# The first two x tiles of a gated two-branch attention kernel: loaded through the DMA crossbar instead of transposed on TensorE, with fewer weight loads and a longer warm-up

## The chip, the cores and the metric

The kernel runs on one core of one Trainium2 chip. The metric is the device time of one execution in microseconds (us). Every execution lists its time, its span and its mean granted TensorE clock, which is given to three digits. On one core no execution here is marked slow; all of those compared are listed as fast.

Each call of experiments ran on one chip together with the kernel before, and kernels are compared within a call.

## The reference, cut to what matters

```python
x = A_x                                    # 1 x 2048 x 1024, bf16
g = sigmoid((x * gate_w).sum(-1, keepdims=True))
a = A_ref(x, A_wqkv, A_wo)                 # linear attention, 32 heads of 32
b = B_ref(x, B_wqkv, B_wo)                 # dilated local attention
return g * a + (1 - g) * b

# in A_ref:
qkv = x @ wqkv
pq, pk = phi(q), phi(k)                    # phi(t) = where(t > 0, t + 1, exp(t)) + 1e-6
```

Only the start matters here: the first work is `pk = phi(x @ wk)` of branch A. The contraction is over the 1024 columns of x, so TensorE needs x transposed: `xT`, with these columns on the partitions.

## The kernel before

x is cut into 16 tiles of 128 rows. Tiles 2 to 15 are transposed by the DMA crossbar on their way in. Tiles 0 and 1 are loaded as rows and transposed on TensorE. The first half of the key weights (`WkA[0]`, 1 MB) comes in eight loads of 128 KB that alternate between two issuing queues, those of SyncE and ScalarE.

```python
load_rows(nc.sync, 0, 1)                   # x tile 0, as rows, 256 KB
load_rows(nc.scalar, 1, 2)                 # x tile 1
WkA = [wpool.tile([P, KT, 512], BF16, name="WkA0", tag="wa")]
for kt in range(KT):                       # KT = 8
    (nc.scalar if kt % 2 else nc.sync).dma_start(out=WkA[0][:, kt, :], in_=A_wqkv[kt * P:(kt + 1) * P, D:D + 512])
for t in range(2, NB):                     # NB = 16
    nc.sync.dma_start_transpose(out=xT[:, :, t * P:(t + 1) * P], in_=rows(x, t * P, (t + 1) * P))
WkA += load_w("WkA", A_wqkv, D, "wa", only=(1,))     # second weight half, 1 MB
load_rows(nc.sync, 2, 4)
...                                        # more rows of x, more weights
warm_up(28)                                # 128x128 matmuls on constants
for t in range(2):
    tp = ps_1.tile([P, KT, P], BF16, name="xt_ps", tag="p1")
    for kt in range(KT):
        nc.tensor.transpose(out=tp[:, kt, :], in_=xrow[:, t, kt * P:(kt + 1) * P], identity=ident[:])
    nc.vector.tensor_copy(out=xT[:, 0:4, t * P:(t + 1) * P], in_=tp[:, 0:4, :])
    nc.scalar.copy(out=xT[:, 4:8, t * P:(t + 1) * P], in_=tp[:, 4:8, :])
warm_up(6)
...
for half in range(2):                      # the projection, L178
    for t0, n in [(0, 2)] + [(t, 1) for t in range(2, NB)]:
        pj = [ps_1.tile([P, 512], F32, name="pk_ps", tag="p1") for _ in range(n)]
        for kt in range(KT):
            for i in range(n):
                t = t0 + i
                nc.tensor.matmul(pj[i][:], lhsT=xT[:, kt, t * P:(t + 1) * P], rhs=WkA[half][:, kt, :],
                                 start=(kt == 0), stop=(kt == KT - 1))
        ...                                # phi of each tile
```

The *next stage* below is `g_ps` (L203): x rows times pk, 256 matmuls. (The expectations call it the third stage.)

Of the kernel before, what the change touches and what calls it, by code (L numbers as in the profile page):

```python
# [7 lines left out]

ACT = mybir.ActivationFunctionType
ALU = mybir.AluOpType  # L10
BF16 = mybir.dt.bfloat16
F32 = mybir.dt.float32
PE = mybir.EngineType.PE
DVE = mybir.EngineType.DVE
P = 128
# [26 lines left out]
def kernel(  # L42
# [11 lines left out]
    nc = tc.nc  # L54
    S, D = A_x.shape[1:]
    assert D == 1024 and S == 2048

    x = A_x[0].rearrange("(m two) d -> two m d", two=2)
    out2 = out[0].rearrange("(m two) d -> two m d", two=2)

    def rows(ap, s0, s1):
        return ap[s0 // 1024, s0 % 1024:(s1 - 1) % 1024 + 1, :]
# [3 lines left out]
    KT = D // P  # L66
    NB = S // P
# [7 lines left out]
    consts = ctx.enter_context(tc.tile_pool(name="consts", bufs=1))  # L75
    wpool = ctx.enter_context(tc.tile_pool(name="wpool", bufs=2))
    dram = ctx.enter_context(tc.tile_pool(name="dram", bufs=1, space=bass.MemoryType.DRAM))
    big = ctx.enter_context(tc.tile_pool(name="big", bufs=1))
# [3 lines left out]
    def load_w(name, src, col0, tag, only=(0, 1)):  # L82
        halves = []
        for h in only:
            w = wpool.tile([P, KT, 512], BF16, name=f"{name}{h}", tag=tag)
            c0 = col0 + h * 512
            nc.sync.dma_start(out=w[:], in_=src[:, c0:c0 + 512].rearrange("(kt p) n -> p kt n", p=P))
            halves.append(w)
        return halves

    xT = big.tile([P, KT, S], BF16, name="xT", tag="xT")
    xrow = big.tile([P, NB, D], BF16, name="xrow", tag="vV")

    def load_rows(eng, t0, t1):
        eng.dma_start(out=xrow[:, t0:t1, :], in_=rows(x, t0 * P, t1 * P).rearrange("(t p) d -> p t d", p=P))

    load_rows(nc.sync, 0, 1)
    load_rows(nc.scalar, 1, 2)
    WkA = [wpool.tile([P, KT, 512], BF16, name="WkA0", tag="wa")]
    for kt in range(KT):  # L100
        (nc.scalar if kt % 2 else nc.sync).dma_start(out=WkA[0][:, kt, :], in_=A_wqkv[kt * P:(kt + 1) * P, D:D + 512])
    for t in range(2, NB):
        nc.sync.dma_start_transpose(out=xT[:, :, t * P:(t + 1) * P], in_=rows(x, t * P, (t + 1) * P))
    WkA += load_w("WkA", A_wqkv, D, "wa", only=(1,))
    load_rows(nc.sync, 2, 4)
    for t in range(4, NB, 4):
        load_rows(nc.sync, t, t + 4)
    WvA = load_w("WvA", A_wqkv, 2 * D, "wb")
# [2 lines left out]
    WqA = load_w("WqA", A_wqkv, 0, "wa")  # L111


    ident = consts.tile([P, P], BF16, name="ident")
    make_identity(nc, ident[:])
    onesb = consts.tile([P, P], BF16, name="onesb")
    nc.vector.memset(onesb[:], 1.0)
    bdmask = consts.tile([P, P], F32, name="bdmask")
# [24 lines left out]
    def phi(dst, pj):  # L143
        e = work.tile([P, 512], F32, name="e", tag="e")
        nc.scalar.activation(out=e[:], in_=pj[:], func=ACT.Exp)  # L145
        nc.vector.tensor_scalar(out=e[:], in0=e[:], scalar1=1.0, scalar2=1e-6, op0=ALU.min, op1=ALU.add)  # L146
        nc.vector.scalar_tensor_tensor(out=dst, in0=pj[:], scalar=0.0, in1=e[:], op0=ALU.max, op1=ALU.add)

    with tc.manual_schedule(engines={PE}):

        with ExitStack() as s1:
            ps_1 = s1.enter_context(tc.tile_pool(name="ps_1", bufs=6, space=bass.MemoryType.PSUM))
            junk = s1.enter_context(tc.tile_pool(name="junk", bufs=1))


            def warm_up(n):
                warm = ps_1.tile([P, P], F32, name="warm", tag="p1")
                for i in range(n):
                    nc.tensor.matmul(warm[:], lhsT=onesb[:], rhs=onesb[:], start=True, stop=True)

            warm_up(28)
            for t in range(2):
                tp = ps_1.tile([P, KT, P], BF16, name="xt_ps", tag="p1")
                for kt in range(KT):
                    nc.tensor.transpose(out=tp[:, kt, :], in_=xrow[:, t, kt * P:(kt + 1) * P], identity=ident[:])  # L165
                nc.vector.tensor_copy(out=xT[:, 0:4, t * P:(t + 1) * P], in_=tp[:, 0:4, :])
                nc.scalar.copy(out=xT[:, 4:8, t * P:(t + 1) * P], in_=tp[:, 4:8, :])
            warm_up(6)

            s1.enter_context(tc.manual_schedule(engines={DVE}))  # L170
            pk = big.tile([P, NB, D], BF16, name="pk", tag="pkO")
            for half in range(2):
                for t0, n in [(0, 2)] + [(t, 1) for t in range(2, NB)]:
                    pj = [ps_1.tile([P, 512], F32, name="pk_ps", tag="p1") for _ in range(n)]
                    for kt in range(KT):
                        for i in range(n):
                            t = t0 + i
                            nc.tensor.matmul(pj[i][:], lhsT=xT[:, kt, t * P:(t + 1) * P], rhs=WkA[half][:, kt, :],  # L178
                                             start=(kt == 0), stop=(kt == KT - 1))
                    for i in range(n):  # L180
                        phi(pk[:, t0 + i, half * 512:(half + 1) * 512], pj[i])

            zacc = junk.tile([P, D], F32, name="zacc", tag="zacc")
            gw_row = junk.tile([P, D], BF16, name="gw_row", tag="gw")
# [12 lines left out]
            for half in range(2):  # L197
                g_ = kq.tile([P, KT, 512], BF16, name=f"G{half}", tag="kq")
                G.append(g_)
                for kt in range(KT):  # L200
                    pj = ps_1.tile([P, 512], F32, name="g_ps", tag="p1")
                    for t in range(NB):
                        nc.tensor.matmul(pj[:], lhsT=xrow[:, t, kt * P:(kt + 1) * P],  # L203
                                         rhs=pk[:, t, half * 512:(half + 1) * 512],
                                         start=(t == 0), stop=(t == NB - 1))
# [12 lines left out]
            for c in range(KT):  # L218
                kvp = ps_1.tile([P, P], F32, name="kv_ps", tag="p1")
                for kt in range(KT):  # L220
                    nc.tensor.matmul(kvp[:], lhsT=WvA[c // 4][:, kt, (c % 4) * P:(c % 4 + 1) * P],  # L221
                                     rhs=G[c // 4][:, kt, (c % 4) * P:(c % 4 + 1) * P],
                                     start=(kt == 0), stop=(kt == KT - 1))
                nc.vector.tensor_tensor(out=KVT[:, c, :], in0=kvp[:], in1=bdmask[:], op=ALU.mult)
            for half in range(2):
                zp = ps_1.tile([P, 512], F32, name="z_ps", tag="p1")
                for i in range(2):
                    nc.tensor.matmul(zp[:], lhsT=onesb[:], rhs=zhl[:, i, half * 512:(half + 1) * 512],  # L228
                                     start=(i == 0), stop=(i == 1))
# [300 lines left out]
```

## Time and profile before

| | before |
|---|---|
| median of three executions | 494.51 us (494.06 to 494.51) |
| span of the profiled execution | 493.0 us |
| first projection matmul starts | 7.51 us |
| granted clock rises to full | 10.38 us |
| first projection of the second weight half starts | 36.56 us |
| first weights of the next stage loaded into PE | 63.97 us |

In the views PE is TensorE, PEld its weight loads, DVE VectorE, ACT ScalarE, POOL GpSimd and SP SyncE; a q behind a name means the engine's instruction queue, for instance while it issues a transfer. L178 is line 178 of the kernel, and x16 counts instructions. Engines wait on semaphores, counters that a finished instruction or transfer raises.

The page of the kernel before: busy time of each engine with its share of the span and its instructions, and the engines of the chain of work that ended last.

```profile
PE 487.6 (99%) x3350; PEld 232.0 (47%) x3350; DVE 283.3 (57%) x550; ACT 181.9 (37%) x281; POOL 7.9 (2%) x28
...
PE 98%; DMA 1%; ACT 0%; issue 0%; ACTq 0%
```

TensorE is the limit from one end to the other. Only the start, where it still waits for data, can give something. The chain of the kernel before in its first 66 us: first the shares by line, then the pieces as start, length and what.

```profile
by line: PE pk_ps L178 85.8%; DMA xrow<-in_A_x_dram 6.6%; PE xt_ps L165 2.9%; PE g_ps L203 2.6%; PE warm L159 1.0%; issue 0.2%
...
0.80 4.34 DMA xrow<-in_A_x_dram
5.14 0.05 issue
5.19 1.89 PE xt_ps L165 x16
7.08 0.64 PE warm L159 x6
7.72 56.63 PE pk_ps L178 x256
```

A load, 16 transposes, six warm-up matmuls, then projections without a gap. The timeline of PE in the kernel before (start, length, what, and in brackets the idle time before it and what ended it):

```profile
1.12 3.17 PE L159 MATMUL warm<-onesb 128*128 128x128 bf16 x28 [1.12 <-DVE onesb L117]
5.19 1.89 PE L165 MATMUL xt_ps<-ident,xrow 128*128 128x128 bf16 x16 [0.91 <-DMA xrow<-in_A_x_dram]
6.87 0.85 PE L159 MATMUL warm<-onesb 128*128 128x128 bf16 x6
7.51 29.21 PE L178 MATMUL pk_ps<-WkA_77,xT 128*128 128x512 bf16 x128
36.56 27.79 PE L178 MATMUL pk_ps<-WkA_100,xT 128*128 128x512 bf16 x128
```

The two halves have the same 128 matmuls, yet the first takes 29.21 us and the second 27.79. The weight loads into PE (PEld) in the kernel before show where the 1.4 us are:

```profile
8.37 0.15 PEld L178 LDWEIGHTS <-xT 128*128 128x128 bf16 x1 [0.27 <-issue]
8.79 0.15 PEld L178 LDWEIGHTS <-xT 128*128 128x128 bf16 x1 [0.27 <-issue]
...
10.45 1.61 PEld L178 LDWEIGHTS <-xT 128*128 128x128 bf16 x8 [0.22 <-issue]
```

Up to 10.45 us a projection starts every 0.43 us, afterwards every 0.216 us: the clock is at half until its rise at 10.38 us. The trace holds that rise. The clock changes on a grid of windows of 3.41 us. Busy time of each engine in stretches of one window, counted back from the rise, in the kernel before (columns: PE, PEld, DVE, ACT and POOL busy us with instructions, PEclk, DMA share, GB/s; the PEclk column gives 1.00 ahead of the first recorded change too, so it is of no use here):

```profile
0.14:3.55 3.41, 2.43 (x24) 2.44 (x25) 0.65 (x6) 1.28 (x1) 2.93 (x18) 1.00 0.41 96
3.55:6.97 3.42, 2.51 (x24) 2.25 (x23) 0.42 (x1) 0.25 (x1) 1.37 (x7) 1.00 0.90 298
6.97:10.38 3.41, 3.41 (x15) 1.61 (x13) 0.42 (x1) 0.92 (x2) 0.00 (x0) 1.00 1.14 165
```

PE was busy for 71%, 73% and 100% of the three windows.

### The profile page before, as it was taken

The page shows a single profiled execution, that of the slowest core. Times are in us where ns is not written, and L with a number is a line of the kernel's source. Part 1 is how long each engine was busy: PE and PEld are TensorE (multiplying, and loading weights), DVE is VectorE, ACT ScalarE, POOL GpSimd, SP SyncE. Part 2 cuts the span into 40 slices and gives each one's busy share as a digit, 9 for nine tenths or more (in the row PEclk, how much of TensorE's full clock was granted, in tenths as well). Part 3 has the DMA queues.
Part 4 walks back from the last instruction along what each step waited for, and adds up shares of the span by engine and source line. Part 5 has one row for each costly group of instructions (what it writes and reads, how often), then busy time and mean ns, then how long its engine had stood idle before and what let it go on. Part 6 is the DMA issues. An engine that isn't in the chain of part 4 may idle for free.

```text
span 493.0 us, 8254 instructions
## 1 busy us (share of the span) xinstructions
PE 487.6 (99%) x3350; PEld 232.0 (47%) x3350; DVE 283.3 (57%) x550; ACT 181.9 (37%) x281; POOL 7.9 (2%) x28
## 2 busy tenths in 40 slices
PE   8999999999999999999999999999999999999997
PEld 5444444446444444444444545454544444444444
DVE  1766689941328999997476767676765397000000
ACT  1333311121543333332455655655655333112121
POOL 3000000000200000000000000000000000000000
PEclk9999999999999999999999999999999999999999
DMA  8999950000621222236011133111164832110101
GB/s 192 163 277 368 348 167 0 1 0 13 206 76 47 93 93 83 66 122 199 3 36 30 32 88 57 30 36 30 36 134 92 208 85 68 60 43 33 43 33 43
DMA packets 78293, 46.03 MB, mean 93 GB/s; under 512 B 51632, under 2 KB 72240, under 8 KB 78256
## 3 DMA queue, kind: packets, MB, share of 16 engines
q1 hardware_dynamic: 77536, 44.73, 33.6%
q10 hardware_dynamic: 720, 0.79, 0.6%
q8 instruction: 26, 0.43, 0.4%
q14 instruction: 11, 0.09, 0.1%
HBM read 21.23 MB, written 7.34 MB: 58 GB/s over the span
## 4 chain that ended last, share of the span: by engine, by line
PE 98%; DMA 1%; ACT 0%; issue 0%; ACTq 0%
PE kq_ps L339 23%; PE d_ps L458 21%; PE pk_ps L178 11%; PE p_ps L262 11%; PE g_ps L203 11%; PE p_ps L296 8%; PE q_ps L296 2%; DMA xrow<-in_A_x_dram 1%; PE kv_ps L221 1%; PE q_ps_4385 L458 1%; PE q_ps L458 1%; PE p_ps L251 1%; PE xt_ps L165 0%; PE q_ps_4266 L296 0%; PE q_ps_4165 L296 0%; PE z_ps L228 0%
## 5 line engine op out<-in xcount | busy, mean ns | idle before, releaser
L203 PE MATMUL g_ps<-pk,xrow 128*128 128x512 bf16 x256 | 55.4, 379 | 0.0
L146 DVE TENSOR_SCALAR e<-e 128x512 f32<-128x512 f32 x64 | 27.2, 424 | 39.9 <-ACT e L145 39.9
L463 ACT ACTIVATE osb<-d_ps,omg 128x512 bf16<-128x512 f32 (+1 forms) x31 | 20.9, 673 | 72.5 <-PE d_ps L458 64.2
L178 PEld LDWEIGHTS <-xT 128*128 128x128 bf16 x256 | 25.4, 99 | 31.0 <-issue 1.8
L458 PEld LDWEIGHTS <-OBT 128*128 128x128 bf16 x264 | 25.7, 98 | 29.2
L203 PEld LDWEIGHTS <-xrow 128*128 128x128 bf16 x256 | 25.0, 98 | 30.2
L262 PEld LDWEIGHTS <-xT 128*128 128x128 bf16 x256 | 25.0, 98 | 30.2
L296 PEld LDWEIGHTS <-xT 128*128 128x128 bf16 x256 | 24.2, 98 | 28.0
L378 DVE TENSOR_TENSOR PT_1893<-PT_1893,mask 128x672 bf16<-128x672 bf16 (+3 forms) x42 | 23.7, 571 | 18.1 <-ACT PT_1893 L376 17.7
L339 PE MATMUL kq_ps<-xT,WkB_1071 128*128 128x512 bf16 x128 | 32.9, 380 | 0.0
L339 PE MATMUL kq_ps<-xT,WqB_1876 128*128 128x512 bf16 x128 | 32.9, 379 | 0.0
L145 ACT ACTIVATE e<-pk_ps 128x512 f32<-128x512 f32 x32 | 18.9, 597 | 37.9 <-PE pk_ps L178 37.9
L339 PE MATMUL kq_ps<-xT,WkB_1069 128*128 128x512 bf16 x128 | 32.3, 379 | 0.0
L339 PE MATMUL kq_ps<-xT,WqB_1874 128*128 128x512 bf16 x128 | 32.2, 379 | 0.0
L378 DVE TENSOR_TENSOR PT_1894<-PT_1894,mask 128x672 bf16<-128x672 bf16 (+3 forms) x40 | 22.3, 565 | 16.8 <-ACT PT_1894 L376 16.5
L345 DVE CAST kqt<-kq_ps 128x512 bf16<-128x512 f32 x32 | 22.0, 687 | 16.5 <-PE kq_ps L339 16.5
L262 PE MATMUL p_ps<-WvB_114,xT 128*128 128x512 bf16 x128 | 30.9, 379 | 0.0
L262 PE MATMUL p_ps<-WvB_116,xT 128*128 128x512 bf16 x128 | 30.9, 379 | 0.0
L458 PEld LDWEIGHTS <-pqT_4443 128*128 128x128 bf16 x200 | 19.6, 98 | 22.1
L267 ACT CAST tmp<-p_ps 128x512 bf16<-128x512 f32 x32 | 18.8, 587 | 30.3 <-PE p_ps L262 30.3
L178 PE MATMUL pk_ps<-WkA_77,xT 128*128 128x512 bf16 x128 | 29.2, 392 | 0.0
L458 PE MATMUL d_ps<-WoB_4080,OBT 128*128 128x512 bf16 (+1 forms) x128 | 28.5, 366 | 0.0
(399 smaller groups left out, 673.6 us busy)
## 6 DMA issues: line engine op xcount, KB each, us to landing
out_dram<-osb SPq DMA_DIRECT2D x31, 128.0 KB, 1.9
xrow<-in_A_x_dram SPq DMA_DIRECT2D x3, 1024.0 KB, 12.0
pqd<-tmp SPq DMA_DIRECT2D x12, 256.0 KB, 2.0
V<-tmp SPq DMA_DIRECT2D x4, 264.0 KB, 2.5
WkA_100<-in_A_wqkv_dram SPq DMA_DIRECT2D x1, 1024.0 KB, 7.2
WvA_106<-in_A_wqkv_dram SPq DMA_DIRECT2D x1, 1024.0 KB, 14.6
WvA_108<-in_A_wqkv_dram SPq DMA_DIRECT2D x1, 1024.0 KB, 15.3
WoA_110<-in_A_wo_dram SPq DMA_DIRECT2D x1, 1024.0 KB, 13.1
```

Source lines behind the costliest of these rows:

```text
L145: nc.scalar.activation(out=e[:], in_=pj[:], func=ACT.Exp)
L146: nc.vector.tensor_scalar(out=e[:], in0=e[:], scalar1=1.0, scalar2=1e-6, op0=ALU.min, op1=ALU.add)
L178: nc.tensor.matmul(pj[i][:], lhsT=xT[:, kt, t * P:(t + 1) * P], rhs=WkA[half][:, kt, :], start=(kt == 0), stop=(kt == KT - 1))
L203: nc.tensor.matmul(pj[:], lhsT=xrow[:, t, kt * P:(kt + 1) * P], rhs=pk[:, t, half * 512:(half + 1) * 512], start=(t == 0), stop=(t == NB - 1))
L262: nc.tensor.matmul(st["pj"][:], lhsT=xT[:, kt, t * P:(t + 1) * P], rhs=WvB[half][:, kt, :], start=(kt == 0), stop=(kt == KT - 1))
L267: nc.scalar.copy(out=v[:, half * 16:(half + 1) * 16, 0:Dh], in_=st["pj"][:].rearrange("p (h e) -> p h e", h=16))
L296: nc.tensor.matmul(st["pj"][:], lhsT=xT[:, kt, t * P:(t + 1) * P], rhs=WqA[half][:, kt, :], start=(kt == 0), stop=(kt == KT - 1))
L339: nc.tensor.matmul(st["pj"][:], lhsT=W[c // 4][:, kt, (c % 4) * P:(c % 4 + 1) * P], rhs=xT[:, kt, cols], start=(kt == 0), stop=(kt == KT - 1))
L345: nc.vector.tensor_copy(out=kqt[:, 1, cols], in_=st["pj"][:])
L378: nc.vector.tensor_tensor(out=ptv[:, hs], in0=ptv[:, hs], in1=m[:, None, :].broadcast_to([P, 2, W_]), op=ALU.mult)
L458: nc.tensor.matmul(st["ps"][:, 0:n], lhsT=lhsT, rhs=W[c0 // 512][:, c, c0 % 512:c0 % 512 + n], start=(side == 0 and c == 0), stop=(side == ...
L463: nc.scalar.activation(out=osb[:, 0:n], in_=st["ps"][:, 0:n], func=ACT.Copy, scale=omg[:, tb:tb + 1])
```

## The change

The intent: take the 16 TensorE transposes and their four copies off the start. Tile 0 comes through the crossbar as the very first transfer, tile 1 between the second and the third quarter of the weights, all on one queue. The weights come in four loads of 256 KB. The projections are ordered as the data should arrive: four of tile 0, four of tile 1, then two each. The warm-up grows from 28 to 36 matmuls. The rows of x for tiles 0 and 1, which the next stage needs, move behind the second weight half.

```diff
-    load_rows(nc.sync, 0, 1)
-    load_rows(nc.scalar, 1, 2)
     WkA = [wpool.tile([P, KT, 512], BF16, name="WkA0", tag="wa")]
-    for kt in range(KT):
-        (nc.scalar if kt % 2 else nc.sync).dma_start(out=WkA[0][:, kt, :], in_=A_wqkv[kt * P:(kt + 1) * P, D:D + 512])
+    nc.sync.dma_start_transpose(out=xT[:, :, 0:P], in_=rows(x, 0, P))
+    for i in range(4):
+        if i == 2:
+            nc.sync.dma_start_transpose(out=xT[:, :, P:2 * P], in_=rows(x, P, 2 * P))
+        nc.sync.dma_start(out=WkA[0][:, 2 * i:2 * i + 2, :],
+                          in_=A_wqkv[2 * i * P:(2 * i + 2) * P, D:D + 512].rearrange("(kt p) n -> p kt n", p=P))
     for t in range(2, NB):
         nc.sync.dma_start_transpose(out=xT[:, :, t * P:(t + 1) * P], in_=rows(x, t * P, (t + 1) * P))
     WkA += load_w("WkA", A_wqkv, D, "wa", only=(1,))
-    load_rows(nc.sync, 2, 4)
+    load_rows(nc.sync, 0, 4)
 ...
-            warm_up(28)
-            for t in range(2):
-                ...  # 8 transposes and 2 copies
-            warm_up(6)
 ...
+            warm_up(36)
+            first = [ps_1.tile([P, 512], F32, name="pk_ps", tag="p1") for _ in range(2)]
+            for t, kts in ((0, (0, 1, 2, 3)), (1, (0, 1, 2, 3)), (0, (4, 5)), (1, (4, 5)), (0, (6, 7)), (1, (6, 7))):
+                for kt in kts:
+                    project(first[t], t, kt, 0)
+                if kts[-1] == KT - 1:
+                    phi(pk[:, t, 0:512], first[t])
```

The rest of the diff drops the identity matrix and rewrites the loop of the other tiles. After the first 16 projections PE executes the same instructions in both kernels, and in the same order but for the first 16 projections of the second weight half: there the kernel before alternates between tiles 0 and 1, and the changed one takes them one after the other. It costs nothing that can be seen (27.79 and 27.80 us for the second half).

## The prediction

> **What bounds the kernel now.** TensorE. The page gives PE 487.6 us busy of a span of 493.0 (99%), and the chain of work that ended last is 98% PE. Only the head can move. There the chain of waits reads: 0.80 to 5.14 us the DMA of the first x rows, 5.19 to 7.08 the 16 transposes on PE, 0.64 us of warm-up matmuls, then from 7.51 us projection matmuls without a gap. After the first two x tiles PE's instruction order is the same in both kernels.
>
> A second limit in the head is the clock. The timeline shows the first projections 0.427 us apart until 10.45 us, then about 0.214. The recorded clock rises to full at 10.38 us, one window of 3.41 us after 6.97. PE's busy time was 2.43 us in 0.14 to 3.55, 2.51 in 3.55 to 6.97, and all of 3.41 in 6.97 to 10.38: only the full window released it. The Trainium skill ("TensorE: Matmul & The Clock Gate", Part 1) describes this: half clock until a busy window of about 3.4 us, free-running. This trace agrees.
>
> **What goes, comes, moves.** Gone: 16 PE transposes (1.89 us), two DVE and two ACT copies (0.42 and 0.58 us each), eight 128 KB weight loads on two queues. Added: two crossbar loads and 8 warm-up matmuls. A crossbar load costs 1.31 us of issue; from issue to landing took 3.9 us at best, 4.5 in the median. The weights become four 256 KB loads, in line behind the first crossbar load. The x rows (0.5 MB) move behind the second weight half.
>
> Estimates from these durations. First crossbar load issued 0.8, landed about 4.9. Quarters 1 and 2 issued from 2.1, landed about 5.6 and 6.4. The second crossbar load is issued at about 3.1, queues behind them, and lands about 8.0 (7.3 to 8.6). Quarters 3 and 4 land about 9.0 and 9.8.
>
> So projections start at about 5.6 instead of 7.51 us, four of them for tile 0, still at half clock; they end about 7.3. Then PE waits about 0.7 us for the second tile. That gap falls into the window 6.97 to 10.38.
> - If the window counts as busy anyway: about 9.6 projections are done at 10.38 instead of 6.7, a gain of 2.9 x 0.214 = 0.6 us. About 45%.
> - If it doesn't: the clock rises at 13.8 us, with about 17.6 projections done instead of 22.7, a loss of 1.1 us. About 55%.
>
> **Critical path.** All 1.9 us of transposes lay on it, yet most of what they free is given back to the wait for the second tile and to the half clock. Later x tiles come every 1.5 us and are used every 1.71; tile 2 should land about 11 us and be needed about 11.8. The second weight half landed at 34.6 and was needed at 36.6; I expect about 34 to 36, so at most some tenths of waiting.
>
> **Prediction: 494.6 us, range 493.0 to 496.0.** Faster by over 2%: 0.5%. Within 2%: 99%. Slower by over 2%: 0.5%.
>
> **What would show each step.** First projection at 5.3 to 6.2 us, released by a DMA. A PE gap of 0.3 to 1.2 us after the fourth projection, ended by the second crossbar load. Time of the clock's rise: 10.4 (gain) or about 13.8 (loss). No other PE gap before 36 us.
>
> **What would make it wrong.** Crossbar and plain loads in one queue slowing each other, so that tile 1 or tile 2 lands over 1 us late; the second weight half late; or a crossbar load of a cold queue landing much before 4.9 us with the clock released early, a gain of 1.5 us or more.

## The result, and the profile after

| | before | after |
|---|---|---|
| median of six executions | 494.51 us (494.06 to 495.10) | 493.09 us (492.66 to 494.60) |
| ratio | | 0.9975 (95% interval 0.996 to 0.999) |
| span of the profiled execution | 493.0 us | 491.1 us |
| first projection | 7.51 us | 5.81 us |
| clock rises | 10.38 us | 6.05 us |
| second weight half, first projection | 36.56 us | 34.92 us |
| next stage, first weights into PE | 63.97 us | 62.34 us |
| last matmul ends | 489.66 us | 488.03 us |

A ratio is the mean time of one kernel's fast runs over that of the other's of the same rounds, so it is not quite the ratio of the medians. The change is within 2%, and faster by 1.4 us. Two further calls gave 0.998 each. The changed kernel has a median of 493.20 us in 18 executions. The two profiled executions took 494.82 and 492.92 us, one above its kernel's median and one below it, so the traces differ by 1.88 us where the medians differ by 1.42.

The page and the chain after, with the same parts as above:

```profile
PE 481.1 (98%) x3276; PEld 230.0 (47%) x3336; DVE 282.8 (58%) x548; ACT 180.6 (37%) x279; POOL 7.6 (2%) x26
...
PE 91%; SPq 5%; DMA 2%; issue 1%; DVE 0%; ACT 0%; ACTq 0%
```

PE's matmul count falls by 74 where the program has 14 fewer (and PEld shows 14); the rest are records missing from the trace, so the busy time of PE is not to be compared to the last microsecond. The chain of the kernel after in its first 66 us (the other pieces, nearly all of the issuing queue, left out):

```profile
by line: PE pk_ps L157 42.0%; SPq L104 30.4%; DMA WkA_96<-in_A_wqkv_dram 12.8%; PE g_ps L202 5.2%; SPq L101 3.1%; SPq L97 2.0%; SPq L100 1.9%; issue 1.8%
...
25.05 1.31 SPq L104
26.35 0.04 issue
26.40 8.47 DMA WkA_96<-in_A_wqkv_dram
34.87 0.05 issue
34.92 7.73 PE pk_ps L157 x35
```

Before, the chain was PE from 5.19 us on. Now, up to 34.9 us, it is the row of crossbar loads (SPq L104 is their issue) and behind them the second weight half: the changed kernel is bound by its loads for its first 35 us. PE and its weight loads in the kernel after:

```profile
1.11 4.02 PE L163 MATMUL warm<-onesb 128*128 128x128 bf16 x36 [1.11 <-DVE onesb L116]
5.81 1.42 PE L157 MATMUL pk_ps<-WkA_75,xT 128*128 128x512 bf16 x4 [0.68 <-DMA WkA_75<-in_A_wqkv_dram]
7.66 26.94 PE L157 MATMUL pk_ps<-WkA_75,xT 128*128 128x512 bf16 x121 [0.42 <-DMA xT<-in_A_x_dram]
34.92 27.80 PE L157 MATMUL pk_ps<-WkA_96,xT 128*128 128x512 bf16 x126 [0.33 <-DMA WkA_96<-in_A_wqkv_dram]
```

```profile
7.65 2.27 PEld L157 LDWEIGHTS <-xT 128*128 128x128 bf16 x12 [0.91 <-DMA xT<-in_A_x_dram]
10.22 23.88 PEld L157 LDWEIGHTS <-xT 128*128 128x128 bf16 x112 [0.30 <-DMA xT<-in_A_x_dram]
34.91 27.31 PEld L157 LDWEIGHTS <-xT 128*128 128x128 bf16 x128 [0.82 <-DMA WkA_96<-in_A_wqkv_dram]
```

Three waits are to be seen: for tile 1 (7.65 us), for tile 2 (10.22 us), and for the second weight half (34.91 us). The windows of the clock in the kernel after, counted back and forward from its rise at 6.05 us (columns as above):

```profile
2.64:6.05 3.41, 2.73 (x25) 2.43 (x23) 0.00 (x0) 0.00 (x0) 1.90 (x10) 1.00 1.05 248
6.05:9.46 3.41, 2.85 (x13) 1.06 (x12) 0.00 (x0) 0.00 (x0) 0.00 (x0) 1.00 1.14 278
```

PE was busy for 80% of the window that ended with the rise. All but one or two of the projections ran at the full clock.

**Where the 1.88 us between the two profiles come from.** The terms are times from the two traces. A projection at full clock takes 0.2157 us, so 16 take 3.45 us.

| step | before | after | gain |
|---|---|---|---|
| first projection starts | 7.51 | 5.81 | 1.70 |
| 16 projections of tiles 0 and 1, beyond 3.45 us: half clock (before), waits and 0.12 us of half clock (after) | 1.43 | 1.00 | 0.43 |
| tile 2 starts (before 12.39, after 10.26) to second half, beyond 112 x 0.2157 us | 0.01 | 0.50 | -0.49 |
| second half starts | 36.56 | 34.92 | 1.64 |
| next stage, first weights | 63.97 | 62.34 | 1.63 |
| end of the last matmul | 489.66 | 488.03 | 1.63 |
| end of the last matmul to end of the span | 3.35 | 3.10 | 0.25 |

Two things stand out. From the next stage to the end of PE's work both kernels take 425.69 us. So all that PE gains is gained in the first 35 us, and 0.25 us more comes from the other end of the kernel, behind the last matmul, where nothing was changed.

### The profile page after: what moved, and what is told of

Its sections match the earlier page's. It is cut to its first block, busy times and chain, and to the rows that moved or that the text cites. A ratio compares the mean times of both kernels' runs of the same rounds, so it can differ in the third digit from the quotient of the medians.

```text
span 491.1 us, 8153 instructions
## 1 busy us (share of the span) xinstructions
PE 481.1 (98%) x3276; PEld 230.0 (47%) x3336; DVE 282.8 (58%) x548; ACT 180.6 (37%) x279; POOL 7.6 (2%) x26
## 4 chain that ended last, share of the span: by engine, by line
PE 91%; SPq 5%; DMA 2%; issue 1%; DVE 0%; ACT 0%; ACTq 0%
PE kq_ps L338 23%; PE d_ps L457 21%; PE g_ps L202 11%; PE p_ps L261 11%; PE p_ps L295 8%; PE pk_ps L157 6%; SPq L104 4%; PE q_ps L295 2%; DMA WkA_96<-in_A_wqkv_dram 2%; PE kv_ps L220 1%; PE q_ps_4355 L457 1%; PE p_ps L250 1%; PE q_ps L457 1%; SPq L101 0%; PE q_ps_4236 L295 0%
## 5 line engine op out<-in xcount | busy, mean ns | idle before, releaser
L338 PE MATMUL kq_ps<-xT,WqB_1846 128*128 128x512 bf16 x120 | 31.8, 379 | 1.0 <-issue 0.6
L338 PE MATMUL kq_ps<-xT,WqB_1844 128*128 128x512 bf16 x124 | 31.7, 379 | 0.7 <-issue 0.5
L338 PE MATMUL kq_ps<-xT,WkB_1041 128*128 128x512 bf16 x122 | 31.6, 379 | 0.2
L338 PE MATMUL kq_ps<-xT,WkB_1039 128*128 128x512 bf16 x120 | 30.7, 379 | 0.4 <-issue 0.2
L157 PE MATMUL pk_ps<-WkA_75,xT 128*128 128x512 bf16 x125 | 28.1, 380 | 1.4 <-DMA WkA_75<-in_A_wqkv_dram 0.7
```

Of the source, the lines that this page charges most:

```text
L157: nc.tensor.matmul(pj[:], lhsT=xT[:, kt, t * P:(t + 1) * P], rhs=WkA[half][:, kt, :], start=(kt == 0), stop=(kt == KT - 1))
L338: nc.tensor.matmul(st["pj"][:], lhsT=W[c // 4][:, kt, (c % 4) * P:(c % 4 + 1) * P], rhs=xT[:, kt, cols], start=(kt == 0), stop=(kt == KT - 1))
```

## The experiments

The theories in dispute:

- *Arrival:* the gain comes from taking the transposes off the chain. Projections start 1.7 us earlier.
- *Clock:* the gain comes from the clock, which rose 4.3 us earlier. The longer warm-up is what did that; how tile 0 gets transposed has no part in it.
- Later, *queue:* the form of the weight loads (eight on two queues, or four on one) is what counts.

All experiments gave correct results. Times inside a run are of its one profiled execution; "tile 2" is its first weight load into PE.

| run | transposes of tiles 0, 1 | warm-up | weight loads | first projection | clock rises | tile 2 | next stage | median of the executions (range), us |
|---|---|---|---|---|---|---|---|---|
| first result: before | TensorE | 28 | 8 | 7.51 | 10.38 | 12.17 | 63.97 | 494.51 (494.06 to 495.10) |
| first result: after | crossbar | 36 | 4 | 5.81 | 6.05 | 10.22 | 62.34 | 493.09 (492.66 to 494.60) |
| *call 1*: before | | | | | | | | 494.62 (493.03 to 495.16) |
| after_again | crossbar | 36 | 4 | 5.81 | 4.01 | 10.68 | 62.83 | 493.30 (492.39 to 494.29) |
| b_warm38 | TensorE | 38 | 8 | 6.30 | 4.24 | 10.68 | 62.48 | 494.05 (493.54 to 494.48) |
| a_warm28 | crossbar | 28 | 4 | 6.00 | 9.55 | 11.05 | 62.85 | 493.93 (493.37 to 494.56) |
| a_fill | crossbar | 44 + 8 | 4 | 6.04 | 6.44 | 10.63 | 62.43 | 493.04 (492.77 to 493.29) |
| *call 2*: before | | | | | | | | 493.84 (493.18 to 494.99) |
| b28_w4 | TensorE | 28 | 4 | 7.53 | 9.05 | 11.52 | 63.32 | 493.96 (492.25 to 494.60) |
| b38_w4 | TensorE | 38 | 4 | 6.99 | 6.42 | 10.37 | 62.17 | 492.84 (492.30 to 493.13) |
| a_lane | crossbar | 36 | 4 | 5.73 | 6.82 | 10.23 | 62.03 | 493.29 (492.47 to 494.30) |
| a_wk1 | crossbar | 36 | 4 | 5.85 | 4.11 | 10.57 | 62.20 | 492.70 (492.61 to 493.37) |
| *call 3*: before | | | | | | | | 494.49 (493.51 to 495.03) |
| c_after | crossbar | 36 | 4 | 5.78 | 4.09 | 10.06 | 62.29 | 493.05 (492.50 to 494.26) |
| c_fill | crossbar | 44 + 8 | 4 | 5.77 | 4.34 | 9.99 | 62.38 | 492.86 (492.42 to 493.09) |
| c_fill_wk1 | crossbar | 44 + 8 | 4 | 5.76 | 3.79 | 10.50 | 62.75 | 493.67 (493.13 to 493.97) |
| c_b38_w4 | TensorE | 38 | 4 | 6.89 | 6.22 | 10.27 | 62.07 | 492.37 (492.10 to 492.87) |

The TensorE variants keep the six warm-up matmuls behind the transposes.

### The changed kernel once more: after_again

No edit.

> The changed kernel once more, so that the others of this call can be compared with it on one chip. Both theories: about 493.1 us, 1.4 below the kernel before. Clock theory: the clock's rise falls at another place in each execution, so single runs scatter by up to 1.7 us (one window of 3.41 us at half clock); arrival theory: no scatter beyond 0.5 us.

Measured 493.30 us, ratio 0.998 (0.996 to 0.9997). The gain repeats, and so does the scatter: 1.9 us between executions, as the clock theory said. The mean granted clock of each execution says more. It does not tell when the clock first rose, since it too counts full clock ahead of the first recorded change, but it shows a later fall. Of this kernel three executions have a mean clock of 0.996, at 494.60, 494.29 and 494.26 us; every other has 0.999 or 1.0, and the median of those is 492.92. One window of 3.41 us at half clock costs 0.35% of the mean (1.7 of 492 us). So in about one execution of six the clock very likely rose and fell back for a window. (The half clock behind the last matmul can't be it: it costs 0.14% at most in the 14 profiles.) None of these three was profiled, so this is read from the mean alone. One execution at 494.21 has a clock of 1.0 and stays unexplained.

### The kernel before with a longer warm-up: b_warm38

```diff
-            warm_up(28)
+            warm_up(38)
```

> The kernel before, with 38 warm-up matmuls in place of 28 and nothing else, so that PE has no pause between warm-up (now to about 5.2 us) and the first transpose at 5.19. Clock theory (the gain comes from the clock that rises at 6 instead of 10.4 us): the clock rises by about 8 us, tile 2 starts at 10.6 to 11.2 us instead of 12.4, about 493.0 us. Arrival theory (the gain comes from the 1.89 us of transposes taken off the chain): within 0.3 us of the kernel before, 494.4 us.

Measured 494.05 us, ratio 0.9994 (0.998 to 1.0007): neither of the two numbers, and no clear gain. The trace shows one thing that the clock theory's 493.0 left out. The clock was up at 4.24 us, and projections started at 6.30, but then (PE of this run):

```profile
6.88 1.89 PE L178 MATMUL pk_ps<-WkA,xT 128*128 128x512 bf16 x8 [0.20 <-issue]
9.60 4.69 PE L178 MATMUL pk_ps<-WkA,xT 128*128 128x512 bf16 x21 [0.83 <-DMA WkA<-in_A_wqkv_dram]
```

PE waited for the sixth slice of the weights. The last two of the eight loads are on ScalarE's queue, and in this trace they are issued only at 5.80 and 6.17 us, since each waits for an earlier transfer, whose semaphore it takes over. They then land at 9.56 and 10.11 us among the crossbar loads, while the sixth of the loads issued earlier had landed at 7.83. At half clock nobody needed them so early: before, PE used the sixth slice after 10.38. A faster PE uncovered the next limit. This gave the queue theory. The wait is not the whole account, though: this profiled execution, wait included, took 493.54 us and began the next stage at 62.48, earlier than after_again (62.83). The other four took 493.98 to 494.48 and were not profiled.

### The changed kernel with the old warm-up: a_warm28

```diff
-            warm_up(36)
+            warm_up(28)
```

> The changed kernel with 28 warm-up matmuls, as many as before, so that PE pauses 1.5 us before the first projection. Clock theory: the clock rises between 9 and 12.6 us, tile 2 starts at about 11.8 instead of 10.2 us, some 1.1 us slower than the changed kernel, about 494.2 us. Arrival theory: as the changed kernel, 493.1 us.

Measured 493.93 us, ratio 0.9992 (0.998 to 1.0004). The median is 0.6 us above after_again's on the same chip, about half of what the clock theory expected. The windows of this run's clock:

```profile
2.72:6.14 3.42, 1.70 (x16) 1.50 (x15) 0.00 (x0) 0.00 (x0) 1.83 (x10) 1.00 0.96 227
6.14:9.55 3.41, 3.41 (x9) 0.90 (x8) 0.00 (x0) 0.00 (x0) 0.00 (x0) 1.00 1.16 267
```

A window that was half busy did not release the clock, and it rose at 9.55 us, between the expected 9 and 12.6. Three of its six executions have a mean clock of 0.996 or 0.997. The direction is that of the clock theory, but this run alone does not settle it: the means differ by 0.56 us with a standard error of 0.36 (estimated from the scatter of the six executions each), and the two profiled executions begin the next stage at 62.85 and 62.83 us. In after_again PE waited for the second weight half, which landed at 35.36 us there and at 34.59 here, and that gave the early clock's gain back. The clearer pair for the warm-up is b28_w4 and b38_w4 below.

### The pauses filled: a_fill and c_fill

```diff
-            warm_up(36)
+            warm_up(44)
 ...
                 for kt in kts:
                     project(first[t], t, kt, 0)
+                if (t, kts[0]) == (0, 0):
+                    warm_up(8)
```

> The changed kernel with 44 warm-up matmuls in place of 36 and 8 more between the first four projections and the second tile's, so that PE has no pause over 0.3 us while it waits for loads. Clock theory: the clock is up by 7 us in every execution, tile 2 starts when its load lands, 10.2 us, and the scatter goes: all runs within 0.5 us of 492.8. Arrival theory: 493.1 us, as the changed kernel.

> The changed kernel with its pauses filled by warm-up matmuls, again. Clock theory: 493.0 us, scatter at most 0.7 us.

Measured 493.04 us in the first call and 492.86 in the third. The range shrinks from 1.9 and 1.8 us (after_again, c_after) to 0.5 and 0.7 us, and no execution has a mean clock below 0.999. That is what the clock theory said, and what the arrival theory has no reason for. It is not proof: if one execution in six falls back, the fifteen filled ones (with c_fill_wk1's five) would all be spared by luck about once in 15 times (an estimate, (5/6) to the 15th). The median gains only 0.2 to 0.3 us: the extra matmuls save the unlucky executions and add nothing to the others, in which the loads set the pace.

### One part alone, the four weight loads: b28_w4

```diff
-    for kt in range(KT):
-        (nc.scalar if kt % 2 else nc.sync).dma_start(out=WkA[0][:, kt, :], in_=A_wqkv[kt * P:(kt + 1) * P, D:D + 512])
+    for i in range(4):
+        nc.sync.dma_start(out=WkA[0][:, 2 * i:2 * i + 2, :],
+                          in_=A_wqkv[2 * i * P:(2 * i + 2) * P, D:D + 512].rearrange("(kt p) n -> p kt n", p=P))
```

> The kernel before with one part of the change alone: the first weight half in four 256 KB loads on one queue, in place of eight on two; TensorE transposes and 28 warm-up matmuls stay. Clock theory: the clock still rises late in most executions (8 to 11 us), the weights are in time anyway, so at most 0.3 us faster than the kernel before, about 494.3 us. Queue theory (the eight loads, of which two wait behind crossbar loads, hold PE up): about 493.3 us in every execution.

Measured 493.96 us, ratio 0.9996 (0.998 to 1.001). The weight loads alone gain nothing that can be seen: in the profile the clock rose only at 9.05 us. One execution of the six came in at 492.25, among the fastest, which fits an early rise; it was not profiled.

### All of the change but the crossbar: b38_w4 and c_b38_w4

The edits of b_warm38 and of b28_w4 together, on the kernel before. Tiles 0 and 1 are still transposed on TensorE.

> The kernel before with 38 warm-up matmuls and the four weight loads, so all of the change but the crossbar itself: the first two x tiles are still transposed on TensorE. If the crossbar is not what gains: no wait at the sixth weight tile (it was 0.83 us with eight loads), tile 2 starts at 10.0 to 10.5 us, the third stage at 62.2 to 62.4, about 492.8 us, as fast as the changed kernel or faster. If the crossbar is what gains (arrival theory): no better than the 494.05 us of the run with 38 warm-ups alone, and 0.7 us slower than the changed kernel.

> TensorE transposes kept, 38 warm-up matmuls, four weight loads, on the same chip as the changed kernel. If the crossbar as such gains nothing: 492.8 us, scatter at most 0.9 us, no slower than any of the other three. If it gains: slower than the filled crossbar version by 0.3 us or more.

Measured 492.84 us in the second call and 492.37 in the third, ratios 0.9976 (0.9965 to 0.9988) and 0.9963 (0.995 to 0.9975). In the second call it differs from b28_w4 by the warm-up alone, and its mean is 1.0 us lower (standard error 0.36, from the scatter); the changed kernel itself was not in that call. In the third call each of its five executions (at most 492.87) is faster than the changed kernel's median of 493.05. Against c_fill the means differ by 0.4 us in its favour while the ranges overlap, so I take it as no slower. The chain of c_b38_w4 in its first 66 us is PE's all the way:

```profile
by line: PE pk_ps L179 83.2%; PE warm L160 6.9%; PE g_ps L204 5.6%; PE xt_ps L166 2.1%; issue 0.9%; DVE onesb L118 0.3%
...
1.12 4.23 PE warm L160 x38
5.35 1.36 PE xt_ps L166 x16
6.72 0.34 PE warm L160 x6
7.05 0.22 PE pk_ps L179
7.27 0.20 issue
7.46 10.74 PE pk_ps L179 x49
```

There is no wait for any load. Its first projection comes 1.1 us later than the changed kernel's (6.89 against 5.78 in c_after), and yet tile 2 starts at nearly the same time (10.27 against 10.06) and the next stage 0.2 us earlier. The landings, worked out from the semaphores of the traces (the last of the 16 increments of each load), tell why:

| landed, us | c_after | c_b38_w4 |
|---|---|---|
| x tile 0 / tile 1 | 4.21 / 7.63 | 4.99 / 5.20 (rows, not yet transposed) |
| weight quarters | 5.74, 6.50, 8.39, 9.11 | 5.92, 6.64, 7.39, 8.15 |
| x tile 2 | 9.91 | 9.04 |
| second weight half | 34.82 (used 34.87) | 32.34 (used about 34.6) |

Behind a full row of transfers a plain 256 KB load adds about 0.75 us, a crossbar load of as many bytes 0.8 to 1.1 us in the opening (tiles 1 and 2), and about 1.5 us in the mean over tiles 3 to 15. In c_after tile 1 was behind the second quarter by 1.13 us. So the two crossbar loads in the opening push the later weights and tile 2 back, by 0.87 us at tile 2. Along the row the delay grows to 2.16 us at tile 15 (30.23 against 28.07) and 2.5 us at the second weight half; that the two more crossbar issues on SyncE, 1.2 to 1.3 us each, account for it is an estimate, which no run tests. The late loads cost about as much as the transposes did on a TensorE that would wait anyway. So the crossbar as such gained nothing here. The longer warm-up, with the early clock that it brings, and the four weight loads did it, and only together: each alone gave 0.9994 and 0.9996.

### The 0.25 us at the end: a_lane

```diff
-            nc.sync.dma_start(out=gw_row[:], in_=gate_w.partition_broadcast(P))
+            for c0, c1 in ((0, 256), (256, 512), (512, 768), (768, 896), (896, 1024)):
+                nc.sync.dma_start(out=gw_row[:, c0:c1], in_=gate_w[c0:c1].partition_broadcast(P))
```

At the end SyncE waits for the semaphores of all transfers in a fixed order, five waits one after the other. The eight semaphores are handed out in turn, so the number of transfers in the whole kernel decides which one the last store has. These are SyncE's steps behind the last store, from the traces (start us, duration ns):

```
before: 490.62 1341 | 492.00 28 | 492.06 28 | 492.13 28 | 492.19 28     the last store is waited for first
after:  488.99   28 | 489.06 28 | 489.12 28 | 490.25 28 | 490.31 28     the last store is waited for fourth
a_lane: 488.68 1286 | 490.00 28 | 490.07 28 | 490.13 28 | 490.19 28     first again
```

> The changed kernel with the gate vector loaded in five pieces in place of one, so four more transfers, which moves the last store from the semaphore that is waited for fourth at the end to one of those waited for first, as in the kernel before. From the end of TensorE's work to the end of the span: 3.34 us as before the change, in place of 3.09. Start of the third stage unchanged, 62.3 to 62.9 us. Time 0.25 us above the changed kernel, about 493.6 us. If the tail's 0.25 us had another cause, it stays at 3.09 us.

From the last matmul's end to the end of the span a_lane takes 3.29 us, against 3.10 after and 3.35 before. So three waits of 0.06 us, which the changed kernel passes while the store is in flight and a_lane after it, 0.19 us, are shown to be the order of the waits; the last 0.06 us is not. b38_w4, with four transfers fewer than before, has its last store in the fourth place too, and 3.12 us. The next stage began at 62.03 us, a little ahead of the expected 62.3. The time of the runs, 493.29 us, is too scattered to show 0.2 us (clock 0.996 and 0.997 in two of six).

### The second weight half ahead of the last tile: a_wk1 and c_fill_wk1

```diff
     for t in range(2, NB):
+        if t == NB - 1:
+            WkA += load_w("WkA", A_wqkv, D, "wa", only=(1,))
         nc.sync.dma_start_transpose(out=xT[:, :, t * P:(t + 1) * P], in_=rows(x, t * P, (t + 1) * P))
-    WkA += load_w("WkA", A_wqkv, D, "wa", only=(1,))
```

> The changed kernel with the load of the second weight half put ahead of the last crossbar load in place of behind it. If that load is what PE waits for at the second half (0.5 to 0.9 us in the two profiles of the changed kernel): it lands by 33.5 us, the second half starts at 34.4 to 34.6 us where tile 2 started at 10.2 to 10.4, the wait goes, and the median falls by 0.3 us to about 493.0. If the last x tile then comes late instead: a wait of up to 0.5 us at tile 15, and no gain.

> Pauses filled and the second weight half ahead of the last crossbar load: the best that I know to make of the crossbar version. 492.8 us, scatter at most 0.7 us, third stage from 62.2 us. If the second weight half is not late once the pauses are filled (tile 2 starts at 10.5 us or later), as the filled run alone, 493.0 us.

On the changed kernel as it is, the trace did what I expected: the half landed at 31.74 us, the wait of PE at the second half went, the median was 492.70. With the pauses filled as well, on another chip, it was 493.67, 0.8 us slower than c_fill on that chip, and neither of the two numbers I had given. The waits of PE's weight loads in that run from 25 to 60 us:

```profile
PEld L158 <- DMA xT<-in_A_x_dram: 0.8, 1, 0.8
```

The half landed at 32.57 and the last x tile behind it at 33.55, while PE wanted it at 32.8. In this execution the row of loads ran so close to its use that the move only shifted the wait from one end of the 1 MB transfer to the other. That does not account for the 0.8 us. The two profiled executions differ by 0.37 us at the next stage, and c_fill_wk1 was already 0.51 us behind at tile 2, ahead of the moved load. c_fill had no wait at the second half (it landed at 33.22), but one of 0.91 us in its weight loads for an x tile at 17.68. What slowed the other executions is open. Whether a_wk1's better median is the order or the chip, these runs do not tell.

### c_after

> The changed kernel, for comparison on the same chip. About 493.3 us, with a scatter of 1.5 to 2 us between executions, since its pauses of 0.7 and 0.4 to 1.0 us let the clock's rise fall where it will.

493.05 us, range 1.8 us, ratio 0.998 (0.9966 to 0.9994); as expected.

## Why the prediction was right or wrong

**Right: the size class and the range.** 493.09 us lies in 493.0 to 496.0 and within 2%. It lies at the lower edge, though: I had put the centre at 494.6, no gain at all, and gave 55% to a loss. That the number fell inside, by 0.09 us, is luck: neither of the two cases that I weighed came true.

**Right: what bounds the kernel, and the arrivals.** The first projection came at 5.81 us (expected 5.6, and 5.3 to 6.2), released by a DMA. The second crossbar load landed at 7.61 us (7.3 to 8.6). PE's pause in front of tile 1 was there, and was ended by that load. Tile 2 landed at 10.18 us (about 11), the second weight half at 34.87 (34 to 36). The first crossbar load landed at 4.19 us, well before the 4.9 of the prediction; the first projection had to wait for the first weight quarter (5.77), so this made no difference there. That PE's order is the same after the first two tiles was not quite so, as said under the change.

**Wrong: the clock. This is the step that failed:** "That gap falls into the window 6.97 to 10.38", and with it the two cases, a rise at 10.4 or at 13.8 us. I had called the windows free-running and then used the ones of a single profile as if they were fixed to the start of the kernel. The 14 profiles have the first rise at 3.79 to 10.38 us. And I had looked only at the pause behind the fourth projection, not at what the eight additional warm-up matmuls do ahead of the first: they lengthen the unbroken busy stretch from 3.17 to 4.02 us. In the profile after, the window of 2.64 to 6.05 was 80% busy, and the clock rose at 6.05. The Trainium skill ("TensorE: Matmul & The Clock Gate", Part 1) says of the window that it is "free-running — it doesn't reset when your kernel starts". The traces agree. In the profile before, the time from the rise (10.38) to the fall at the end (491.66) is 141.0 windows of 3.413 us, and the phase of that grid differs from profile to profile. With the same four weight loads, ten more warm-up matmuls took 1.0 us off the mean (b38_w4 against b28_w4); on the changed kernel a_warm28 points the same way, and no filled execution showed a fallen clock. The case that I had listed last, a gain of 1.5 us or more with the clock released early, comes nearest to what happened, but it was the warm-up that released it.

**Wrong in size: the wait for the second weight half.** I had allowed "at most some tenths"; it was 0.50 us of lost projection time. Tile 2 started 2.1 us earlier, but the loads did not.

**Missed: the end of the kernel,** 0.25 us, of which 0.19 is the order of the waits for the transfers. I had not counted how many transfers the kernel makes.

**The intent of the change was wrong too, in part.** Taking the transposes off TensorE starts the projections 1.7 us earlier, but the crossbar loads take their place in the row of transfers. The kernel that keeps the transposes and takes the rest of the change is no slower (492.84 and 492.37 us).

**Open:** why b_warm38's unprofiled executions lie 0.4 to 0.9 us above its profiled one; what happened in the executions with a mean clock of 0.996, which no trace caught; why all five executions of c_fill_wk1 were slower than those of c_fill; the last 0.06 us of the end.

## What to carry to other kernels

At the start of a kernel count the bytes and transfers ahead of each thing that TensorE needs, and leave work on TensorE that would only wait otherwise: a transpose moved into a full row of loads delays everything behind it. Keep the warm-up unbroken up to the first real matmul and across the first waits; in this kernel the time of the clock's rise otherwise depended on chance. Look at several executions and at the mean clock of each before you believe a gain of a microsecond. Where two changes lift one limit each (clock, weight loads), neither shows anything alone; try them together before you drop one.

## What the Trainium skill lacked or had wrong

- **"TensorE: Matmul & The Clock Gate", Part 1** gives the window's length and says that it must be busy, not how busy. In 14 profiles every window that ended with the first rise had PE busy for 78% to 100%, and every earlier window for at most 73%. So the limit lay between 73% and 78% of busy time as these traces model it. The transposes on TensorE count for it: b28_w4's window of 5.63 to 9.05 us was 94% busy and ended with the rise, and without its transposes it would be 57%, less than the 71% that did not release the clock in the kernel before. After a rise, windows of 52% to 54% (after_again, a_wk1, c_after) did not bring the clock down again; the window that ended with the fall behind the last matmul was at most 41% busy in all 14.
- **"DMA: Bandwidth & Descriptors", Issuing engines are not separate DMA queues**, says that several issuing engines save only issue time. It does not speak of the wait for a reused semaphore. In b_warm38, with eight loads on two queues, this wait held two of them until 5.80 and 6.17 us; they landed at 9.56 and 10.11 us, and PE waited 0.83 us. Four loads on one queue had all landed by 8.25 us (b38_w4). The runs do not separate the number of queues from the number of loads (ten transfers ahead of the tiles for eight semaphores, against six).
- **"DMA: Bandwidth & Descriptors", Latency and other measured facts**, gives 261 GB/s for crossbar transposes, measured on one kernel, and more in its contiguous case. Here 13 loads of 256 KB landed between 10.18 and 29.12 us in the profile after, 1.46 us each or 180 GB/s. Each takes 1.2 to 1.3 us of SyncE's issue at least, and the first one of the kernel took 3.4 us from issue to landing. At that issue time, one queue can't pass about 200 GB/s with loads of this size (an estimate: 256 KB in 1.3 us), so this is no measure of what the crossbar itself can do. The page has no time of one such load.
- No page that I read has the waits at the end of a kernel: 0.06 us for each semaphore still to be passed behind the one of the last store, 3.29 (a_lane) against 3.10 us. The three profiles with 195 transfers have 3.29 to 3.35 us from the last matmul to the end of the span, the eleven with 191 have 3.08 to 3.12.
